# Reordering one projection step and the closing tiles of a fused attention and gating kernel

## The chip, the cores and the metric

The kernel runs on one core of a Trainium2 chip, as one launch. The metric is the device time of that launch in microseconds (us); less is better. The engines are named as the profile names them: PE (TensorE matmul), PEld (its weight loads), DVE (VectorE), ACT (ScalarE), POOL (GpSimd) and SP (SyncE, which here only issues DMAs).

## The reference

```python
xn = layernorm(A_x)                                   # 2048 x 640
# A: attention, 32 heads of 192, over the last W = 512 keys of the cache
q = (xn @ wq).heads()                                 # wq 640 x 6144
k, v = k_cache[:, :, -512:], v_cache[:, :, -512:]
p = softmax(q @ k.T * 192 ** -0.5)
s = (p @ v).merge_heads() @ wo                        # wo 6144 x 640
# B: two tokens (top 2 of xn @ w_r) go through a gated MLP; the others pass
b = xn; b[top2] += mlp(xn[top2]) * sigmoid(r[top2])
out = A_x + s * silu(b)                               # bfloat16
```

## The kernel before, in words

Every engine's instructions stand in an order that is written out by hand; the program's order of calls is the order on each engine's queue.

**Work items.** Heads are taken in 8 groups of four, and a group in two pairs of heads. A step is (group, 512 tokens, pair), 64 steps; each step has four token tiles of 128, so there are 256 items `m`, numbered through. For one `m` the kernel makes:

- scores (`scores`, L335 to L344): two heads, each a 128x512 bank of PSUM;
- the row maxima (`row_max`, L353, DVE), the exponentials (`exps`, L361, ACT, which also sum the rows) and a transpose of the exponentials by DMA, issued by SP (L366, `pT<-pexp`);
- P V (`o_products`, L378: 8 matmuls of 192 columns), whose result DVE scales by the reciprocal row sums into `o_sb` (`o_scaled`, L393), and a DMA transpose of `o_sb` (`o_turned`, L399, `oT<-o_sb`).

Beside these run two projections: `q_item` (L294), 5 matmuls of 512 columns for a third of a step's q, evacuated by ACT (L299); and `w_item`, the product with wo for 128 tokens of one group (`w_products`, L419: 12 matmuls of 320 columns in two halves), which DVE adds to `s_acc` (L437), or in the last group multiplies by the gate (`fin_t`, L442) and adds to `s_acc` (`fin_o`, L444). In the last stretch POOL also folds the gate and the residual into `s_acc` (L850, L851).

**PSUM.** `f_tile` deals out two banks in turn; q and P V both take them, so each user waits until the one before the last is evacuated. `w_banks` is one pair of banks for the wo product and for the scores of the first `m` of a unit. Four banks hold the other scores.

**Order.** From item 24 on the `m` are taken three at a time; such a triple is a unit `U` (12 to 88; unit 89 holds item 255 alone). For units 12 to 87 a loop plays the tokens of one string, STRETCH (L860): after the unit's scores, `M0` to `M5` are its six row maxima, `E0` to `E2` the exponentials of its three items, `R` the reciprocals of the unit before, `O1` one P V (of items one unit back), `q1` one q item, `W1` one wo product; `q`, `O`, `W` without a number are what is left of each (a unit has 3 P V, 2 or 3 q items, 1 or 2 wo products), `m`, `n`, `b` are pieces of part B, and `l` the loads. The exponentials of a unit's first two items share one transpose, which SP issues after `E1`; the third has its own after `E2`. The second P V of a unit reads the transpose that the unit before issued after its `E1`.

The closing part is a second string, LAST, played by `last` (L903): tokens `S`, `M`, `E`, `R` as above, `O.m` the P V matmuls of item `m`, `o.m` its scaling, `W.k` the wo product of token tile `k` in its last group (119 to 127; `.w` in `w_banks`, `.t` in a pair of banks that the scores have left, `.h` in an `f_tile` bank), `m.k` the product with the gate on DVE (L950), `g.k` or `a.k` the last addition on POOL or DVE (L954) and the store by SP (L955). `o` issues a transpose of its own item, except for items 252 and 255, which PE transposes (`T`, L411) and ACT copies (L413). `C` frees the score banks.

Of the kernel before, what the change touches and what calls it, by code (L numbers as in the profile page):

```python
# [9 lines left out]
ALU = mybir.AluOpType  # L10
AX = mybir.AxisListType
ET = mybir.EngineType
FP32 = mybir.dt.float32
BF16 = mybir.dt.bfloat16
# [7 lines left out]
def kernel(ctx, tc, A_x, A_k_cache, A_v_cache, A_wq, A_wo, B_x, B_w_r, B_w_gate, B_w_up, B_w_down, out):  # L22
    nc = tc.nc
    P = 128
    _, S, D = A_x.shape
# [3 lines left out]
    W = min(4096, max(256, Sk // 4))  # L29
# [9 lines left out]
    PAIRS = GROUP // 2  # L39
    CPG = GROUP * Dh // P  # L40
    DA = 512
    HD = D // 2
# [7 lines left out]
    out_v = out.flatten_outer_dims().rearrange("(n p) d -> p n d", p=P)  # L50
# [22 lines left out]
    def f_tile(shape, dtype, name):  # L73
        return ps_f.tile(shape, dtype, name=name, tag="f")

    xn = big.tile([P, NTB, D], BF16, name="xn")
    xnT = big.tile([P, NTB, DC, P], BF16, name="xnT")
    s_acc = big.tile([P, NTB, D], FP32, name="s_acc")
# [66 lines left out]
    for _ in range(22):  # L145
# [5 lines left out]
        out=ident_f, in_=ident_f, compare_op=ALU.not_equal, fill=1.0, base=0,  # L151
# [119 lines left out]
    steps = [(g, t5, pr) for g in range(NG) for t5 in range(NT5) for pr in range(PAIRS)]  # L271
    NS = len(steps)
    NM = 4 * NS
# [42 lines left out]
    def w_banks():  # L316

        if not wb:
            wb.extend(ps_w.tile([P, W], FP32, name=f"w_{c}", tag=f"w{c}") for c in range(2))
        return wb  # L320

    def scores(U):

        ms = units[U]
        tiles = {}
        for m in ms[1:] + ms[:1] if len(ms) == 3 else ms:
            g, t5, pr = steps[m // 4]
            ssl = slice((m % 4) * P, (m % 4 + 1) * P)
            if len(ms) == 3 and m == ms[0]:
                s0, s1 = w_banks()  # L330
            else:
                s0 = ps_sc.tile([P, W], FP32, name="s0", tag="sc")
                s1 = ps_sc.tile([P, W], FP32, name="s1", tag="sc")
            qT, kp = qT_of[m // 4], grp[g]["kT"][:, pr]
            nc.tensor.matmul(s0, lhsT=qT[:, 0, ssl], rhs=kp[:, :, 0, :], start=True, stop=False)  # L335
            nc.tensor.matmul(s1, lhsT=qT[:, 2, ssl], rhs=kp[:, :, 2, :], start=True, stop=False)  # L336
            tiles[m] = (s0, s1)
        for m in ms:
            g, t5, pr = steps[m // 4]
            ssl = slice((m % 4) * P, (m % 4 + 1) * P)  # L340
            s0, s1 = tiles[m]
            qT, kp = qT_of[m // 4], grp[g]["kT"][:, pr]
            nc.tensor.matmul(s0, lhsT=qT[0:64, 1, ssl], rhs=kp[0:64, :, 1, :], start=False, stop=True)  # L343
            nc.tensor.matmul(s1, lhsT=qT[64:128, 1, ssl], rhs=kp[64:128, :, 1, :], start=False, stop=True)  # L344
        return [tiles[m] for m in ms]
# [23 lines left out]
    def recip(U):  # L369
        n = 2 * len(units[U])  # L370
        nc.vector.reciprocal(out=l_of[U][:, 0:n], in_=l_of[U][:, 0:n])

    def o_products(m):
        g, t5, pr = steps[m // 4]
        o_ps = f_tile([P, 2, Dh], FP32, "o_ps")
        for hh in range(2):
            for j in range(NJ):
                nc.tensor.matmul(o_ps[:, hh, :], lhsT=pT_ring[:, m % RP, hh, j, :], rhs=grp[g]["v"][:, 2 * pr + hh, j, :],  # L378
                                 start=(j == 0), stop=(j == NJ - 1))
        return o_ps  # L380

    def o_slot(m):
        return (m if m < 2 * HEAD - 4 else m + 1) % RO

    def o_scaled(m, o_ps, act=False):
        U, a = unit_of[m]
        o_sb = o_ring[:, o_slot(m)]
        ls = l_of[U][:, 2 * a:2 * a + 2]
        if act:
            for hh in range(2):  # L390
                nc.scalar.activation(out=o_sb[:, hh], in_=o_ps[:, hh, :], func=ACT.Copy, scale=ls[:, hh:hh + 1])
        else:
            nc.vector.tensor_tensor(out=o_sb, in0=o_ps, in1=ls.unsqueeze(2).to_broadcast([P, 2, Dh]), op=ALU.mult)  # L393

    def o_turned(ms):

        n = len(ms)
        a, b = o_slot(ms[0]), (ms[0] + 1) % RT
        nc.sync.dma_start_transpose(out=oT_ring[:, b:b + n].rearrange("p u c t -> p (u c) t"),  # L399
                                    in_=o_ring[:, a:a + n].rearrange("p u h d -> p (u h d)"))  # L400
# [14 lines left out]
    def w_products(b, u, w_ps, part, off=0):  # L415

        wo_g = grp[steps[b * PAIRS][0]]["wo"]
        for c in range(CPG):
            nc.tensor.matmul(w_ps[:, part.start - off:part.stop - off], lhsT=oT_ring[:, (8 * b + 4 * (c // 3) + u + 1) % RT, c % 3, :],  # L419
                             rhs=wo_g[:, c, part], start=(c == 0), stop=(c == CPG - 1))  # L420

    fin_pool = {}
    tail_banks = []
# [168 lines left out]
    M = {}  # L592
# [264 lines left out]
        bg[109 + n].append(fin_pre(n))  # L857


    STRETCH = "M0 M1 R O1 E0 q1 M2 M3 E1 O1 M4 M5 E2 W1 m q1 n W q O b l".split()  # L860
    for token in FIRST:
        first(token)
    def q_until(s):
# [5 lines left out]
    for U in range(HEAD, NU - 2):  # L869
# [13 lines left out]
        tiles = scores(U)  # L883
        for token in STRETCH:
            if token[0] == "M":
# [14 lines left out]
    tail_ps = {}  # L900
    tail_sb = {}

    def last(token):  # L903


        op, *n = token.split(".")
        if op == "O":
            tail_ps[token[1:]] = o_products(int(n[0]))
        elif op == "o":
            o_scaled(int(n[0]), tail_ps[token[1:]])  # L910
            if int(n[0]) not in (NM - 4, NM - 1):
                o_turned([int(n[0])])
        elif op == "T":
            o_turn([int(m) for m in n])
        elif op == "R":
            recip(int(n[0]))
        elif op == "S":
            last_tiles[int(n[0])] = scores(int(n[0]))
        elif op == "M":
            row_max(int(n[0]), last_tiles[int(n[0])], int(n[1]))  # L920
        elif op == "E":
            exps(int(n[0]), int(n[1]), last_tiles[int(n[0])])
        elif op == "C":
            score_banks.close()
            tail_banks.append(pool("ps_t", 2, space=bass.MemoryType.PSUM))
        else:
            b, u = divmod(int(n[0]), 4)
            half = n[1] if len(n) > 1 and n[1] in "01" else None
            cs = slice(0, D) if half is None else slice(int(half) * HD, (int(half) + 1) * HD)
            g, t5, _ = steps[b * PAIRS]  # L930
            tok = t5 * 4 + u
            key = token[1:]
            if op == "W":
                key = "." + ".".join(n[:-1])
                if n[-1] == "t":
                    w_ps = tail_banks[0].tile([P, 2, W], FP32, name="w_t", tag="t")
                    w_ps = [w_ps[:, h, 0:HD] for h in range(2)]
                elif n[-1] == "w":
                    w_ps = [t[:, 0:HD] for t in w_banks()]
                else:  # L940
                    w_ps = {int(half): f_tile([P, HD], FP32, "w_e")}
                for h in range(2) if half is None else (int(half),):
                    w_products(b, u, w_ps[h], slice(h * HD, (h + 1) * HD), h * HD)
                tail_ps[key] = w_ps
            elif op == "m":
                if half is None or ("t", tok) not in tail_sb:
                    tail_sb["t", tok] = fin_pool["t"].tile([P, D], FP32, name="fin_t")
                for h in range(2) if half is None else (int(half),):
                    hs = slice(h * HD, (h + 1) * HD)
                    nc.vector.tensor_tensor(out=tail_sb["t", tok][:, hs], in0=tail_ps[key][h], in1=xn[:, tok, hs], op=ALU.mult)  # L950
            else:
                if half is None or ("o", tok) not in tail_sb:
                    tail_sb["o", tok] = fin_pool["o"].tile([P, D], BF16, name="fin_o")
                (nc.gpsimd if op == "g" else nc.vector).tensor_tensor(out=tail_sb["o", tok][:, cs], in0=tail_sb["t", tok][:, cs], in1=s_acc[:, tok, cs], op=ALU.add)  # L954
                nc.sync.dma_start(out=out_v[:, tok, cs], in_=tail_sb["o", tok][:, cs])  # L955

    LAST = """
    S.88 M.88.0 M.88.1 R.87 O.248 o.248 E.88.0 O.249 o.249 M.88.2 M.88.3 E.88.1 W.119.w m.119 O.250 o.250 M.88.4 M.88.5 E.88.2 g.119 W.120.w m.120 g.120 O.251 o.251
    S.89 M.89.0 M.89.1 E.89.0 R.88 C W.121.w m.121 g.121 O.252 o.252 W.122.w O.253 o.253 m.122 T.252 g.122 O.254 o.254 W.123.w m.123 g.123 R.89
    W.124.t m.124 g.124 O.255 o.255 W.125.w m.125 g.125 T.255 W.126.t m.126 g.126 W.127.0.h W.127.1.h m.127.0 m.127.1 a.127.0 a.127.1  # L960
    """.split()
    for token in LAST:
        last(token)
# [31 lines left out]
```

## Time and profile before

| what | us |
|---|---|
| three timed runs | 808.7, 811.0, 809.54 (median 809.54) |
| the profiled execution: its own time | 807.38 |
| its span in the trace | 805.6 |
| PE, busy with matmuls | 790.8 |
| DVE, busy | 624.1 |
| ACT, busy | 500.2 |
| POOL, busy | 217.4 |

The span is the time from the first instruction to the last in the trace of one execution; the execution's own time is 1.8 us more, for what lies around it. A busy PE is one with a matmul in its pipeline: matmuls overlap, so how densely they follow is read from the distance of their starts. The granted TensorE clock of the execution was 0.999 of full speed.

### The profile page before, as it was taken

Reading aid. Unit: us, or ns where it says so; the run is one execution under the profiler, and the core shown is the slowest. Engines: PE = TensorE matmul, PEld = TensorE weight load, DVE = VectorE, ACT = ScalarE, POOL = GpSimd, SP = SyncE. Lnnn points to the kernel's source line nnn. Section 1 sums busy time; section 2 is a strip of 40 time slices with the busy share of each in tenths; the row PEclk is TensorE's granted clock in tenths of the full one; section 3 lists DMA queues with packets and bytes.
Section 4 is the critical chain, followed back from the end, with each engine's and each line's share of the span. In section 5 each row is a group of like instructions: output and inputs, shape, how many; then the busy total and the mean of one; then the engine's idle time right before and its main releaser. Section 6 shows DMA issues by size and latency. Waiting matters only on the chain.

```text
span 805.6 us, 15848 instructions
## 1 busy us (share of the span) xinstructions
PE 790.8 (98%) x5776; PEld 483.2 (60%) x5776; DVE 624.1 (77%) x1303; ACT 500.2 (62%) x1281; POOL 217.4 (27%) x175
## 2 busy tenths in 40 slices
PE   8899999999999999999999999999999999999997
PEld 4456566666566665665665666666665565656665
DVE  7988778887787766777776777678888877668895
ACT  5777655665566665566655566557776666556651
POOL 0112000000000000000003899999900002452554
PEclk9999999999999999999999999999999999999999
DMA  8998999999799998899997996788888899897996
GB/s 219 189 176 167 195 203 168 173 174 189 160 203 195 200 198 162 187 199 191 206 184 151 188 199 138 154 174 174 172 159 152 164 183 188 166 156 145 176 156 133
DMA packets 441678, 142.31 MB, mean 177 GB/s; under 512 B 414500, under 2 KB 441256, under 8 KB 441600
## 3 DMA queue, kind: packets, MB, share of 16 engines
q1 hardware_dynamic: 439936, 138.79, 90.0%
q0 software_dynamic: 720, 1.70, 0.8%
q8 instruction: 45, 0.74, 0.4%
q10 hardware_dynamic: 944, 0.82, 0.3%
q14 instruction: 33, 0.27, 0.1%
HBM read 39.98 MB, written 2.62 MB: 53 GB/s over the span
## 4 chain that ended last, share of the span: by engine, by line
PE 89%; DMA 4%; DVE 3%; ACT 2%; issue 1%; DVEq 0%; SPq 0%; ACTq 0%
PE w L419 24%; PE q_ps L294 23%; PE o_ps L378 20%; PE s L336 4%; PE s L335 4%; PE s L343 4%; DMA pT<-pexp 4%; PE w L343 3%; PE w L335 2%; PE w L336 2%; DVE nm L353 2%; ACT pexp L361 1%; PE warm_ps L146 1%; DVE o_sb L393 0%; PE tp L267 0%
## 5 line engine op out<-in xcount | busy, mean ns | idle before, releaser
L361 ACT ACTIVATE pexp<-s,nm 128x512 bf16<-128x512 f32 x358 | 242.3, 684 | 14.9 <-DVE nm L353 10.5
L361 ACT ACTIVATE pexp<-w,nm 128x512 bf16<-128x512 f32 x154 | 104.5, 683 | 229.7 <-DVE nm L353 229.6
L353 DVE TENSOR_REDUCE nm<-s 128x1 f32<-128x512 f32 x358 | 228.6, 679 | 4.5 <-PE s L344 3.7
L294 PE MATMUL q_ps<-xnT,wq_g 128*128 128x512 bf16 x945 | 230.4, 379 | 0.1
L419 PE MATMUL w<-wo_g,oT 128*128 128x320 bf16 x1500 | 224.2, 299 | 0.0
L378 PE MATMUL o_ps<-v_sb,pT 128*128 128x192 bf16 x2048 | 211.1, 246 | 4.6 <-DMA pT<-pexp 3.2
L378 PEld LDWEIGHTS <-pT 128*128 128x128 bf16 x2048 | 169.1, 98 | 74.1 <-issue 36.6
L419 PEld LDWEIGHTS <-oT 128*128 128x128 bf16 x1536 | 148.6, 98 | 58.7 <-issue 0.9
L393 DVE TENSOR_TENSOR o_sb<-o_ps,lsum 128x384 bf16<-128x384 f32 x249 | 135.1, 543 | 55.5 <-PE o_ps L378 54.7
L353 DVE TENSOR_REDUCE nm<-w 128x1 f32<-128x512 f32 x154 | 99.1, 685 | 66.1 <-PE w L344 66.1
L294 PEld LDWEIGHTS <-wq_g 128*128 128x128 bf16 x945 | 91.0, 98 | 80.3 <-issue 1.1
L299 ACT ACTIVATE qT<-q_ps 128x512 bf16<-128x512 f32 x178 | 106.3, 597 | 22.2 <-PE q_ps L294 14.8
L437 DVE TENSOR_TENSOR s_acc<-s_acc,w 128x320 f32<-128x320 f32 x192 | 86.3, 479 | 28.1 <-PE w L419 28.0
L361 ACT ACTIVATION_READ_ACCUMULATOR pexp<-s,nm 128x1 f32 x358 | 72.0, 201 | 0.0
L336 PE MATMUL s<-kT,qT 128*128 128x512 bf16 x179 | 67.8, 379 | 1.4 <-ACT pexp L361 0.9
L335 PE MATMUL s<-kT,qT 128*128 128x512 bf16 x179 | 67.9, 379 | 0.6 <-ACT pexp L361 0.6
L794 POOL TENSOR_SCALAR yh<-y_bc,oh 128x640 bf16<-128x640 bf16 x32 | 60.5, 1892 | 2.9 <-DMA y_bc<-y_d 1.3
L780 POOL DMA_DIRECT2D y<-yp x4 | 2.1, 524 | 214.3 <-ACT yp L774 214.2
L343 PE MATMUL s<-kT,qT 64*128 64x512 bf16 x179 | 53.2, 377 | 0.0
L344 PE MATMUL s<-kT,qT 64*128 64x512 bf16 x179 | 53.2, 377 | 0.0
L343 PEld LDWEIGHTS <-qT 64*128 64x128 bf16 x256 | 17.1, 94 | 48.4 <-issue 38.4
L795 POOL TENSOR_TENSOR xn<-xn,yh 128x640 bf16<-128x640 bf16 x32 | 44.7, 1396 | 2.7
(148 smaller groups left out, 532.7 us busy)
## 6 DMA issues: line engine op xcount, KB each, us to landing
wo_g<-in_A_wo_dram SPq DMA_DIRECT2D x48, 160.0 KB, 2.9
wq_g<-in_A_wq_dram SPq DMA_DIRECT2D x35, 192.0 KB, 2.9
k_raw<-in_A_k_cache_dram SPq DMA_DIRECT2D x32, 192.0 KB, 3.4
v_sb<-in_A_v_cache_dram SPq DMA_DIRECT2D x32, 192.0 KB, 3.2
pT<-pexp SPq DMA_TRANSPOSE x169, 4.3
x_fin<-in_A_x_dram SPq DMA_DIRECT2D x16, 160.0 KB, 2.7
wgu<-in_B_w_gate_dram SPq DMA_DIRECT2D x15, 128.0 KB, 3.1
wgu<-in_B_w_up_dram SPq DMA_DIRECT2D x15, 128.0 KB, 3.1
```

The source lines that it names most:

```text
L294: nc.tensor.matmul(q_ps, lhsT=grp[g]["wq"][:, dc, col0:col0 + P], rhs=xnT[:, t5 * 4:(t5 + 1) * 4, dc, :], start=(dc == 0), stop=(dc == DC ...
L299: nc.scalar.activation(out=qT_of[i][:, c, :], in_=q_ps, func=ACT.Copy, scale=scale)
L335: nc.tensor.matmul(s0, lhsT=qT[:, 0, ssl], rhs=kp[:, :, 0, :], start=True, stop=False)
L336: nc.tensor.matmul(s1, lhsT=qT[:, 2, ssl], rhs=kp[:, :, 2, :], start=True, stop=False)
L343: nc.tensor.matmul(s0, lhsT=qT[0:64, 1, ssl], rhs=kp[0:64, :, 1, :], start=False, stop=True)
L353: nc.vector.tensor_reduce(out=nm_of[U][:, c:c + 1], in_=tiles[c // 2][c % 2], axis=AX.X, op=ALU.max, negate=True)
L361: nc.scalar.activation(out=p_ring[:, slot, hh, :], in_=tiles[a][hh], func=ACT.Exp, bias=nm_of[U][:, c:c + 1], scale=1.0, accum_out=l_of[U] ...
L378: nc.tensor.matmul(o_ps[:, hh, :], lhsT=pT_ring[:, m % RP, hh, j, :], rhs=grp[g]["v"][:, 2 * pr + hh, j, :], start=(j == 0), stop=(j == NJ ...
L393: nc.vector.tensor_tensor(out=o_sb, in0=o_ps, in1=ls.unsqueeze(2).to_broadcast([P, 2, Dh]), op=ALU.mult)
L419: nc.tensor.matmul(w_ps[:, part.start - off:part.stop - off], lhsT=oT_ring[:, (8 * b + 4 * (c // 3) + u + 1) % RT, c % 3, :], rhs=wo_g[:, ...
L437: nc.vector.tensor_tensor(out=s_acc[:, n, cs], in0=s_acc[:, n, cs], in1=w_ps[:, 0:HD], op=ALU.add)
L794: nc.gpsimd.tensor_scalar(out=yh, in0=M["y_bc"][:, j, :], scalar1=M["oh"][:, n, j:j + 1], scalar2=None, op0=ALU.mult)
```

## The change

1. In STRETCH the second `O1` and the `q1` behind the first wo product change places: the order scores, P V, q, P V, wo, q, ... becomes scores, P V, q, q, wo, P V, ... In each of the 76 units of the loop the second P V is issued behind the second q item and the wo product, and its scaling on DVE behind that of the wo product; ACT evacuates the second q item between `E1` and `E2`. SP's order in the loop is the same as before.
2. LAST is rewritten. Scaling and transposing are separate tokens (`o` and `U`): the closing items are transposed by DMA three, three and two at a time (248 to 250, 251 to 253, 254 and 255), and the PE transposes and ACT copies are gone. P V of two items stand together ahead of a wo product. The additions of tiles 120 and 122, of the first half of tile 126 and of the second part of tile 127 are on DVE, the others on POOL.
3. Stores are tokens of their own (`s`) and are issued by POOL (tiles 119, 121, 122), ACT (120, 123, 124, last part of 127) and SP (125, 126, first part of 127); before, all by SP.
4. The last tile is split in 384 and 256 columns, before in 320 and 320.

```diff
-    STRETCH = "M0 M1 R O1 E0 q1 M2 M3 E1 O1 M4 M5 E2 W1 m q1 n W q O b l".split()
+    STRETCH = "M0 M1 R O1 E0 q1 M2 M3 E1 q1 M4 M5 E2 W1 O1 m n W q O b l".split()
...
         elif op == "o":
             o_scaled(int(n[0]), tail_ps[token[1:]])
-            if int(n[0]) not in (NM - 4, NM - 1):
-                o_turned([int(n[0])])
+        elif op == "U":
+            o_turned([int(m) for m in n])
...
+            lc = LC if k == 4 * NS // PAIRS - 1 else HD
+            parts = [slice(0, lc), slice(lc, D)]
...
+            elif op in "ag":
+                if ("o", tok) not in tail_sb:
+                    tail_sb["o", tok] = fin_pool["o"].tile([P, D], BF16, name="fin_o")
+                (nc.gpsimd if op == "g" else nc.vector).tensor_tensor(out=tail_sb["o", tok][:, cs], in0=tail_sb["t", tok][:, cs],
+                                                                      in1=s_acc[:, tok, cs], op=ALU.add)
             else:
...
-                nc.sync.dma_start(out=out_v[:, tok, cs], in_=tail_sb["o", tok][:, cs])
+                queue = {"s": nc.sync, "p": nc.gpsimd, "a": nc.scalar}[n[-1]]
+                queue.dma_start(out=out_v[:, tok, cs], in_=tail_sb["o", tok][:, cs])
 
     LAST = """
-    S.88 M.88.0 M.88.1 R.87 O.248 o.248 E.88.0 O.249 o.249 M.88.2 M.88.3 E.88.1 W.119.w m.119 O.250 o.250 M.88.4 M.88.5 E.88.2 g.119 W.120.w m.120 g.120 O.251 o.251
-    S.89 M.89.0 M.89.1 E.89.0 R.88 C W.121.w m.121 g.121 O.252 o.252 W.122.w O.253 o.253 m.122 T.252 g.122 O.254 o.254 W.123.w m.123 g.123 R.89
-    W.124.t m.124 g.124 O.255 o.255 W.125.w m.125 g.125 T.255 W.126.t m.126 g.126 W.127.0.h W.127.1.h m.127.0 m.127.1 a.127.0 a.127.1
+    R.87 S.88 O.248 M.88.0 M.88.1 O.249 M.88.2 M.88.3 o.248 o.249 E.88.0
+    W.119.w O.250 E.88.1 M.88.4 M.88.5 O.251 o.250 m.119 S.89 M.89.0 E.88.2 M.89.1 g.119 s.119.p U.248.249.250
+    W.120.w E.89.0 C m.120 o.251 a.120 O.252 s.120.a
+    W.121.w R.88 R.89 O.253 o.252 m.121 o.253 O.254 g.121 s.121.p o.254
+    W.122.w m.122 O.255 a.122 U.251.252.253
+    W.123.w s.122.p o.255 m.123 U.254.255
+    W.124.w g.123 s.123.a m.124 g.124
+    W.125.t m.125
+    W.126.w m.126.0 s.124.a g.125 a.126.0 m.126.1 g.126.1 s.125.s
+    W.127.0.h m.127.0 s.126.s
+    W.127.1.h g.127.0 m.127.1 a.127.1 s.127.1.a s.127.0.s
     """.split()
```

More of the change, by code (lines that the diff above doesn't have):

```diff
@@ L901 @@
     tail_sb = {}
+    LC = 384
     def last(token):
@@ L926, in last @@
         else:
[L927 to L932, printed above, removed]
+            k = int(n[0])
+            b, u = divmod(k, 4)
+            tok = steps[b * PAIRS][1] * 4 + u
+            half = int(n[1]) if len(n) > 1 and n[1] in "01" else None
+            lc = LC if k == 4 * NS // PAIRS - 1 else HD
@@ L933, in last @@
+            parts = [slice(0, lc), slice(lc, D)]
+            cs = slice(0, D) if half is None else parts[half]
+            hs = range(2) if half is None else (half,)
             if op == "W":
-                key = "." + ".".join(n[:-1])
                 if n[-1] == "t":
-                    w_ps = tail_banks[0].tile([P, 2, W], FP32, name="w_t", tag="t")
-                    w_ps = [w_ps[:, h, 0:HD] for h in range(2)]
+                    w_t = tail_banks[0].tile([P, 2, W], FP32, name="w_t", tag="t")
+                    w_ps = [w_t[:, h] for h in range(2)]
@@ L938, in last @@
                 elif n[-1] == "w":
-                    w_ps = [t[:, 0:HD] for t in w_banks()]
+                    w_ps = w_banks()
                 else:
[L941 to L944, printed above, removed]
+                    w_ps = {half: f_tile([P, W], FP32, "w_e")}
+                for h in hs:
+                    w_products(b, u, w_ps[h], parts[h], parts[h].start)
+                    tail_ps[k, h] = w_ps[h]
@@ L945, in last @@
             elif op == "m":
-                if half is None or ("t", tok) not in tail_sb:
+                if ("t", tok) not in tail_sb:
                     tail_sb["t", tok] = fin_pool["t"].tile([P, D], FP32, name="fin_t")
-                for h in range(2) if half is None else (int(half),):
-                    hs = slice(h * HD, (h + 1) * HD)
-                    nc.vector.tensor_tensor(out=tail_sb["t", tok][:, hs], in0=tail_ps[key][h], in1=xn[:, tok, hs], op=ALU.mult)
-            else:
-                if half is None or ("o", tok) not in tail_sb:
-                    tail_sb["o", tok] = fin_pool["o"].tile([P, D], BF16, name="fin_o")
-                (nc.gpsimd if op == "g" else nc.vector).tensor_tensor(out=tail_sb["o", tok][:, cs], in0=tail_sb["t", tok][:, cs], in1=s_acc[:, tok, cs], op=ALU.add)
-                nc.sync.dma_start(out=out_v[:, tok, cs], in_=tail_sb["o", tok][:, cs])
+                for h in hs:
+                    nc.vector.tensor_tensor(out=tail_sb["t", tok][:, parts[h]], in0=tail_ps[k, h][:, 0:parts[h].stop - parts[h].start],
+                                            in1=xn[:, tok, parts[h]], op=ALU.mult)
+            elif op in "ag":
[3 more added lines that the diff above has]
+                                                                      in1=s_acc[:, tok, cs], op=ALU.add)
+            else:
+                queue = {"s": nc.sync, "p": nc.gpsimd, "a": nc.scalar}[n[-1]]
+                queue.dma_start(out=out_v[:, tok, cs], in_=tail_sb["o", tok][:, cs])
```

## The prediction

> **What bounds the kernel now.** I read the page first, for the shares of the engines.
>
> ```profile
> span 805.6 us, 15848 instructions
> ...
> PE 790.8 (98%) x5776; PEld 483.2 (60%) x5776; DVE 624.1 (77%) x1303; ACT 500.2 (62%) x1281; POOL 217.4 (27%) x175
> ```
>
> PE decides. Whether 98% leaves anything shows in the distance of matmul starts in the timeline: 0.216 us within q, 0.136 within wo, 0.083 within P V, the same in nearly every pair of neighbours between 104 and 776 us. The change adds and takes away no matmul there, so only places where PE stands still can be gained. The waits of PE and of its weight loads between 83 and 776 us name them (columns: total, times, longest):
>
> ```profile
> PEld L378 <- DMA pT<-pexp: 6.2, 9, 1.2
> ...
> PE o_ps L378 <- DMA pT<-pexp: 1.9, 5, 0.7
> PE o_ps L378 <- DVE o_sb L393: 0.7, 1, 0.7
> ```
>
> All of it is P V (L378). The timeline of one such unit shows which of the three:
>
> ```profile
> 378.67 1.24 PE L294 MATMUL q_ps<-xnT,wq_g 128*128 128x512 bf16 x5
> 380.61 0.83 PE L378 MATMUL o_ps<-v_sb,pT 128*128 128x192 bf16 x8 [0.70 <-DMA pT<-pexp]
> 381.28 1.79 PE L419 MATMUL w<-wo_g,oT 128*128 128x320 bf16 x12
> ```
>
> It is the second P V, behind the first q item. Five q starts take 1.08, so it could have begun at 379.75: 0.86 lost. (The view says 0.70, since it counts from the modelled end of a matmul.) By starts, seven units lose time to the transpose: at 287 us 0.54, 305 0.35, 379 0.86, 390 0.04, 671 0.57, 707 0.18, 744 0.42, together 2.96. Two more, at 643 (0.83) and 571 (0.08), have another cause:
>
> ```profile
> 642.80 1.24 PE L294 MATMUL q_ps<-xnT,wq_g 128*128 128x512 bf16 x5
> 644.71 0.82 PE L378 MATMUL o_ps<-v_sb,pT 128*128 128x192 bf16 x8 [0.67 <-DVE o_sb L393]
> ```
>
> Here the transpose had landed; the PSUM bank was still held by the first P V, because DVE was late with its scaling.
>
> Last the end, by the chain in order of time:
>
> ```profile
> 788.84 0.67 PE o_ps L378 x8
> ...
> 790.77 4.24 DMA pT<-pexp
> 795.05 0.83 PE o_ps L378 x8
> ...
> 797.52 0.17 PE tp_o L411 x3
> ...
> 801.41 0.93 DVE fin_o L954
> ```
>
> By starts PE loses 0.49 before item 254 and 0.96 before item 255, and each PE transpose takes 0.17. After the last matmul come two gate products, two additions, and the last store, issued at 802.92.
>
> **The stretch, units 12 to 87.** The order of instructions of the changed kernel shows the second P V moved on PE and its scaling on DVE in each unit, and SP's queue unchanged, so transposes and loads pass nothing new there. The matmuls per unit are the same.
>
> - The second P V starts 1.08 (q) + 1.63 (wo) = 2.7 us later. The longest late landing is 0.86, so the 2.96 goes. The third P V reads the same transpose and comes later still.
> - The second q item takes the old place of the second P V and the same bank, so it waits for the first P V's scaling as that did: the 0.83 and the 0.08 stay. Counted as nothing.
> - ACT evacuates the second q (597 ns, L299) between `E1` and `E2`. `E1` is not moved. The next user of that bank is the third q or the third P V. At 449.53 us, for example, it is a P V; `E1` is through at 448.2, the evacuation would end at 448.8, and P V finds the bank free. Over all units that slack comes to 0.60 us or more. `E2` moves back by up to 0.6; the next unit's scores need its bank at 450.84 there, and it would be through at 450.3. Hidden; if the cover is gone, each 0.1 us beyond it costs 7.6 us over 76 units.
> - DVE's row maxima `M4`, `M5` come one scaling earlier (0.46 apart in the queue), so the evacuation of wo, which they held up (PE gives its last matmul 0.42 later than before), ends as before. Whatever wo product follows needs the first bank 0.55 or more after that: hidden.
> - Behind the wo evacuation now waits the second scaling. In the last group `fin_o` (0.82) stands ahead of it. This bites only in unit 85, the one unit there with three q items: its third P V would start at 758.48, the bank comes free at about 758.86. Price +0.38.
>
> Stretch: -2.96 + 0.38 = -2.6.
>
> **The end, from the scores of unit 88 (775.54 in the old frame).** I laid the new order out by hand with the distances of starts above, 0.2 us from a matmul's last start to DVE, and on DVE 0.60 a row maximum, 0.52 a scaling, 0.40 a gate half and 0.82 an addition.
>
> - PE: P V 248, 249, wo 119, P V 250, 251, scores 89 end at 783.01. wo 120 needs the first `w` bank, which DVE, now with `M.88.4`, `M.88.5` and a scaling ahead of `m.119`, frees at 783.27: +0.26.
> - The transposes of 252 to 255 no longer queue behind four single transposes of `o_sb` (1.2 us each of SP, L399). With 3.2 us from issue to landing as in the closing part before, they land at 783.4, 784.8, 786.5 and 789.1; their P V come at 784.9, 787.2, 787.9 and 790.1. The 0.49 and the 0.96 go, and the two times 0.17 of PE transposes.
> - DVE, with the additions of 120 and 122, scales 255 only at 792.2 and frees the first bank for wo 124 at 792.66, PE being ready at 792.43: +0.25. The joint transpose of 251 to 253 is issued at 789.1. Nearest rows: 2.3 (three blocks) to 5.3 (nine blocks under load); I take 3.3, as the page's median says. It is needed at 793.1; at 5.3 it costs +1.3.
> - wo 127 then ends at 799.17 against 800.80: PE -1.6.
> - The additions on DVE beside POOL. The trace has this addition alone and beside one of POOL:
>
> ```profile
> 757.72 0.82 DVE L444 TENSOR_TENSOR fin_o<-fin_t,s_acc 128x640 bf16<-128x640 f32 x1
> ```
> ```profile
> 749.69 1.40 POOL L850 TENSOR_TENSOR s_acc<-s_acc,xn 128x640 f32<-128x640 f32 x1
> 750.25 1.54 DVE L444 TENSOR_TENSOR fin_o<-fin_t,s_acc 128x640 bf16<-128x640 f32 x1
> ```
>
> The second ends 0.70 after POOL's (751.09), and in the chain above the half addition of 0.93 ends 0.34 after POOL's (802.00), where its twin alone takes 0.48. So I let such an addition end 0.34 after POOL's. `a.126.0`, ready at 797.55, meets `g.125` (797.12 to 798.66) and ends at 799.0; behind it on DVE wait `m.126.1`, `m.127.0`, `m.127.1` (800.3). `a.127.1` meets `g.127.0` (800.35 to 801.27) and ends at 801.55. The stores leave at 801.35 and 801.6, against 802.92.
>
> The Trainium skill, page "SBUF — State Buffer", section "Who interferes with whom", calls the port that VectorE and GpSimd share an exclusive lock: a VectorE operation with two SBUF inputs and a GpSimd operation that reads SBUF never share it, and the loser waits for the whole instruction. The trace agrees (0.70 and 0.34 behind POOL's end). If both were merely slowed to 0.93 a half, the same layout would issue the last store at about 800.9, and the end would gain 2.0 instead of 1.2.
>
> - The last store on ACT's queue: the closing stores of SP landed 1.6 to 2.0 after issue; a load of ACT's queue, under load at the start, 4.0. I take 1.7, the row nearest in kind and place; the other end costs +2.3. Stores by POOL (0.58 of POOL each) are early, and no one waits for them.
>
> End: 802.92 - 801.6 = 1.3, less 0.1 for the queue: -1.2.
>
> **Sum.** -2.6 - 1.2 = -3.8. The profiled execution took 807.38 (span 805.6, the rest lies around it): 803.6. The timed runs lie higher, median 809.54, and I forecast in their frame: 805.7.
>
> **Rivals.**
> - The waits come back elsewhere. The busy share of the DMA engines between 83 and 300 us is 0.98; if they and not the place of one P V limit the rate, a gap closed here opens at another transpose. The end's 1.2 alone is left: 808.3. Against it: where PE does not wait, the landings come 0.3 to 4.2 us ahead of need and do not drift.
> - More waits than profiled. The median run is 2.2 us longer than the profiled one; if that is late landings, they go too: 803.5. For it: such waits are irregular. Against: nothing shows where those 2.2 lie.
> - The end gives back. The store on ACT's queue lands in 4.0: -3.8 + 2.3, 808.0.
> - Slower: the bank of the second q. Its slack of 0.60 is alike in all units, so one common delay of the evacuation behind `E1` hits all 76. It decides from 0.6 us; at 0.7 the price is 7.6, and 809.54 - 3.8 + 7.6 = 813.3. For it: ACT takes three q and exponentials in a row where it had two, and every one waits for DVE. Against: neither `E1` nor what it waits for moves.
> - That the change does not do what it says can be excluded: the order on the engines shows it.
>
> **How the numbers follow.** Runs of one kernel differ by about 0.3% (2.4 us; 808.7 to 811.0 here), which bounds "the same". Forecast (804.3 to 807.1) 0.50; more waits gone (803.5) 0.15; waits come back (808.3) 0.14; the end gives back (808.0) 0.11; slower 0.10. Faster: the first two and a part of the third and fourth that noise carries over, 0.68; same 0.21; slower 0.11. The range 803.2 to 808.6 takes in all but the slower case and the outer half of the second.
>
> **What would show it.** In the changed profile: no wait of L378 for `pT` between 83 and 776 us, and PE's span from the first scores of unit 12 to those of unit 88 shorter by 2.6; the wait for `o_sb` near 643 us now before a q matmul; about 0.38 of wait in unit 85; the last matmul 1.6 earlier against unit 88's scores; L958 on DVE stretched twice beside POOL; the last store near -1.3. It is wrong if waits for q's bank (ACT L299) appear in every unit, or if waits for DMA show before other matmuls.

## The result, and the profile after

| | before | after |
|---|---|---|
| timed, median (us) | 809.45 (808.7 to 811.0, 6 runs) | 805.60 (805.21 to 806.74, 6 runs) |
| profiled execution (us), its span | 807.38, 805.6 | 805.67, 803.9 |

The ratio is 0.9952, with a 95% interval of 0.9939 to 0.9965: 3.85 us faster, where 3.8 was forecast (805.7). The two profiled executions differ by 1.7 only.

The changed kernel's page opens as before's did; columns are busy time, share and instructions:

```profile
span 803.9 us, 15821 instructions
...
PE 790.2 (98%) x5770; PEld 483.7 (60%) x5770; DVE 643.8 (80%) x1305; ACT 486.3 (60%) x1279; POOL 217.6 (27%) x177
```

PE is as busy as it was; what can have changed is where it stands still. Its waits in the changed kernel between 83 and 776 us (total, times, longest), which answer to before's 6.2 + 1.9 for `pT`:

```profile
PE q_ps L294 <- DVE o_sb L393: 0.6, 2, 0.5
PE o_ps L378 <- DMA pT<-pexp: 0.5, 1, 0.5
PE o_ps L378 <- DVE o_sb L393: 0.3, 1, 0.3
```
```profile
PEld L378 <- DMA pT<-pexp: 0.9, 1, 0.9
```

The late transposes are gone but for one, and that one is unit 12's first P V at 87 us, which the change does not move. The wait for the first scaling has moved from P V (L378) to q (L294). It is the old one, at the same place; in the changed kernel's timeline:

```profile
642.29 1.24 PE L294 MATMUL q_ps<-xnT,wq_g 128*128 128x512 bf16 x5
644.00 1.24 PE L294 MATMUL q_ps<-xnT,wq_g 128*128 128x512 bf16 x5 [0.46 <-DVE o_sb L393]
```

By starts, 1.71 less 1.08 for five q matmuls, it is 0.63. DVE is late there because its gate operation (L802), beside POOL, took 1.77 and ended at 642.2, ahead of the unit's first maxima and that scaling.

To see where the time went I cut each trace at three matmuls: the first scores of unit 12, those of unit 88, and the first of wo 127 (us):

| kernel | start to unit 12 | unit 12 to 88 | unit 88 to wo 127 | wo 127 to the end |
|---|---|---|---|---|
| before | 83.69 | 691.85 | 23.63 | 6.43 |
| before, a second profile (e5) | 83.84 | 693.78 | 23.57 | 6.41 |
| after | 84.30 | 689.85 | 23.11 | 6.64 |
| stretch alone (e1) | 84.90 | 689.56 | 23.56 | 6.48 |
| end alone (e2) | 84.00 | 693.76 | 22.51 | 6.63 |
| tiles 119, 120 not stored (e3) | 84.72 | 690.24 | 21.82 | 6.72 |
| late stores, two more additions on DVE (e8) | 83.61 | 689.21 | 22.22 | 5.96 |

The code up to unit 12 is the same in all, and takes 83.6 to 84.9 here (85.6 in e7): a single profile decides nothing below 1 to 2 us over its whole span. The stretch gained 2.00 against before's first profile and 3.93 against its second, where 2.6 was forecast. The six profiles with the new stretch and the rest of the loop unchanged (after, e1, e3, e4, e7, e8) lie at 689.2 to 690.2, the three with the old one at 691.9 to 693.8. The end gained 0.31 (23.63 + 6.43 - 23.11 - 6.64), where 1.2 was forecast; in e2 it gained 0.92. Why the end gave so little is in its chain, in order of time:

```profile
784.51 5.52 DMA pT<-pexp
790.03 0.04 issue
790.07 0.83 PE o_ps L378 x8
790.90 3.26 PE w L419 x24
794.16 1.64 PE w_t L419 x12
...
795.90 0.77 DVE fin_t L953 x2
...
797.24 1.17 DVE fin_o L958
```

The transpose of item 255 was issued early (784.51), but took 5.52 to land, where the forecast had 3.2. PE stood 1.45 for it (by starts), more than the 0.96 that the change was to take away here. Below the last line the addition on DVE, which waits for POOL's, leads on to POOL's two additions of the last tiles (799.29 to 801.28) and to the last store behind them.

### The profile page after: what moved, and what is told of

It is laid out like the page before. It is cut to its first block, busy times and chain, and to the rows that moved or that the text cites. A ratio compares the mean times of both kernels' runs of the same rounds, so it can differ in the third digit from the quotient of the medians.

```text
span 803.9 us, 15821 instructions
## 1 busy us (share of the span) xinstructions
PE 790.2 (98%) x5770; PEld 483.7 (60%) x5770; DVE 643.8 (80%) x1305; ACT 486.3 (60%) x1279; POOL 217.6 (27%) x177
## 5 line engine op out<-in xcount | busy, mean ns | idle before, releaser
L353 DVE TENSOR_REDUCE nm<-s 128x1 f32<-128x512 f32 x358 | 222.6, 680 | 4.5 <-PE s L344 3.6
L294 PE MATMUL q_ps<-xnT,wq_g 128*128 128x512 bf16 x945 | 222.0, 379 | 0.7 <-DVE o_sb L393 0.6
L378 PE MATMUL o_ps<-v_sb,pT 128*128 128x192 bf16 x2048 | 207.6, 246 | 2.5 <-DMA pT<-pexp 1.7
L378 PEld LDWEIGHTS <-pT 128*128 128x128 bf16 x2048 | 169.1, 98 | 53.5 <-issue 36.0
L294 PEld LDWEIGHTS <-wq_g 128*128 128x128 bf16 x945 | 90.6, 98 | 89.0 <-issue 2.8
L299 ACT ACTIVATE qT<-q_ps 128x512 bf16<-128x512 f32 x178 | 106.9, 600 | 24.2 <-PE q_ps L294 16.9
L437 DVE TENSOR_TENSOR s_acc<-s_acc,w 128x320 f32<-128x320 f32 x192 | 92.7, 487 | 35.2 <-PE w L419 32.4
L361 ACT ACTIVATION_READ_ACCUMULATOR pexp<-s,nm 128x1 f32 x358 | 77.2, 216 | 0.0
```

The lines of the kernel that those rows point to most:

```text
L294: nc.tensor.matmul(q_ps, lhsT=grp[g]["wq"][:, dc, col0:col0 + P], rhs=xnT[:, t5 * 4:(t5 + 1) * 4, dc, :], start=(dc == 0), stop=(dc == DC ...
L299: nc.scalar.activation(out=qT_of[i][:, c, :], in_=q_ps, func=ACT.Copy, scale=scale)
L353: nc.vector.tensor_reduce(out=nm_of[U][:, c:c + 1], in_=tiles[c // 2][c % 2], axis=AX.X, op=ALU.max, negate=True)
L361: nc.scalar.activation(out=p_ring[:, slot, hh, :], in_=tiles[a][hh], func=ACT.Exp, bias=nm_of[U][:, c:c + 1], scale=1.0, accum_out=l_of[U] ...
L437: nc.vector.tensor_tensor(out=s_acc[:, n, cs], in0=s_acc[:, n, cs], in1=w_ps[:, 0:HD], op=ALU.add)
```

## The experiments

Each ratio is to the kernel before, timed in turn on the same chip. Where it has no interval, there was one run.

### The two halves

**e1**, STRETCH as changed, LAST and all else as before:

```diff
-    STRETCH = "M0 M1 R O1 E0 q1 M2 M3 E1 O1 M4 M5 E2 W1 m q1 n W q O b l".split()
+    STRETCH = "M0 M1 R O1 E0 q1 M2 M3 E1 q1 M4 M5 E2 W1 O1 m n W q O b l".split()
```

> The kernel before with the new order of the stretch and the old end. Theory A (the moved P V brings most): 2.0 to 3.5 us faster than before, no wait of L378 for pT left in units 13 to 87, and the end as before (PE's last product about 23.6 us behind the first scores of unit 88). Theory B (the end brings most): within 1.2 us of before.

Measured: 806.24 against 808.78, ratio 0.9961 [0.9949, 0.9974], 3.2 us by the ratio (2.5 by the medians). In its profile the only wait of L378 for `pT` in the loop is unit 12's, and unit 88 to wo 127 is as before, 23.56. Theory A holds.

**e2**, LAST as changed with its code, STRETCH as before (the diff above, reversed, on the changed kernel).

> The old order of the stretch with the new end. Theory A: 0.5 to 1.2 us faster than before, the waits of the second P V for pT as numerous as before. Theory B: 2.5 us faster or more. If the two parts are independent, the two gains add up to the 3.85 of the whole change.

Measured: 808.19, ratio 0.9989 [0.9979, 0.9998], 0.9 us (0.6 by the medians). The sum, 4.1 (3.1), agrees with the whole's 3.85 within the intervals, so nothing shows that the halves touch each other, and the stretch brings most.

### What before's profile did not show

**e5**, the kernel before, unchanged, profiled once more.

> The kernel before, unchanged, profiled a second time. The measured gain by the timed runs is 3.85 us, by the two profiled executions only 1.7. Theory M (the first profiled execution had few late landings): starts of the second P V in units 12 to 87 lose 4.0 us or more to the transpose of pexp, against 2.96 in the first profile. Rival N (the 2 us lie at the start or the end): they lose 2.5 to 3.3 and the difference shows before unit 12 or behind the scores of unit 88.

Measured: 809.41, span 807.6. Its waits between 83 and 776 us:

```profile
PE o_ps L378 <- DMA pT<-pexp: 3.3, 5, 0.9
```
```profile
PEld L378 <- DMA pT<-pexp: 8.2, 10, 1.4
```

They were 1.9 and 6.2. By starts, eight units lose 4.47 to a late transpose, where seven lost 2.96 in the first profile. Theory M holds. In e2, whose stretch is also the old one, it is 4.40. Counted by unit, the places are nearly the same in all three (us lost before the second P V):

| unit | 32 | 34 | 36 | 40 | 44 | 45 | 76 | 80 | 84 |
|---|---|---|---|---|---|---|---|---|---|
| before | - | 0.54 | 0.35 | - | 0.86 | 0.04 | 0.57 | 0.18 | 0.42 |
| e5 | 1.08 | 0.34 | 0.22 | - | 1.02 | 0.19 | 1.05 | 0.15 | 0.42 |
| e2 | - | 0.49 | 0.56 | 0.25 | 1.58 | - | 0.94 | 0.17 | 0.41 |

The times in the trace differ (unit 44's is at 380.61 in one trace, at 381.88 in the next), the units do not. So where a transpose lands late is set by the program; how late, and whether a close one tips over, differs from run to run. Unit 32's landed 0.09 ahead of need in the first profile. In the seven units of the first profile these transposes took 5.3 to 7.3 us to land, in most others 4.3 to 4.6; some others took over 5.3 and were still in time. What slows them was not tested. The first profile, of a run 1.3 us below the shortest timed one beside it (807.38 against 808.7), lost little. That is 1.5 of the 2.0 us between the two profiles, and most of why the timed gain is larger than the difference of the two first profiles.

### Why item 255's transpose took 5.5

Around it, in the changed kernel, POOL's and ACT's queues hold stores of tiles 119 and 120 (first time: issue). The transpose's issue on SP, with what stands near it on POOL and ACT:

```profile
784.51 1.36 SPq L366 DMA_TRANSPOSE pT<-pexp  x1
```
```profile
784.02 0.56 POOL L962 DMA_DIRECT2D out_dram<-fin_o  x1 [0.30 <-POOL fin_o L958]
```
```profile
785.32 9.75 ACTq L962 DMA_DIRECT2D out_dram<-fin_o  x2
```

Theory S: these stores, which the change issues early, slow the transposes beside them. Theory Q: the joint transpose of `o_sb` for 248 to 250 ahead of it on SP's queue does.

**e3** leaves out the stores of tiles 119 and 120, so those rows of the output are not written:

```diff
-    W.119.w O.250 E.88.1 M.88.4 M.88.5 O.251 o.250 m.119 S.89 M.89.0 E.88.2 M.89.1 g.119 s.119.p U.248.249.250
-    W.120.w E.89.0 C m.120 o.251 a.120 O.252 s.120.a
+    W.119.w O.250 E.88.1 M.88.4 M.88.5 O.251 o.250 m.119 S.89 M.89.0 E.88.2 M.89.1 g.119 U.248.249.250
+    W.120.w E.89.0 C m.120 o.251 a.120 O.252
```

> The changed kernel without the stores of tiles 119 and 120 (their rows of the output are left out). It asks why the transpose of item 255 took 5.5 us to land in the changed kernel where 3.2 was predicted, which holds PE up by 1.37 us. Theory S (the stores issued by POOL and ACT at 783.8 and 785.1 compete with it): it lands 3.2 to 3.6 us after its issue and the wait of PE before item 255 falls to 0.2 or less. Theory Q (it stands behind the joint transpose of 248 to 250 in one queue of DMAs): landing 5.0 to 5.6 and a wait of 1.2 to 1.4, as in the changed kernel.

Measured: 805.25. The transpose lands 3.21 after its issue, and P V of 255 follows without a wait:

```profile
789.43 0.82 PE L378 MATMUL o_ps<-v_sb,pT 128*128 128x192 bf16 x8
```

Unit 88 to wo 127 takes 21.82, against 23.11. The joint transpose stands ahead as it did, so alone it does not make item 255's late: theory S holds, Q as the only cause does not.

**e4** keeps the stores and splits the joint transpose, so that less stands ahead:

```diff
-    ... g.119 s.119.p U.248.249.250
-    W.120.w E.89.0 C ...
+    ... o.248 o.249 E.88.0 U.248.249
+    ... g.119 s.119.p
+    W.120.w E.89.0 U.250 C ...
```

> The changed kernel with the transpose of 248 to 250 taken apart: 248 and 249 together between the transposes of 252 and 253, 250 alone behind that of 254. Theory Q: the transpose of 255 lands about 4 us after issue, the wait before item 255 falls from 1.37 to 0.5 or less, and the run is 0.6 to 1.2 us faster than the changed kernel (4.5 to 5.0 faster than before). Theory S: the wait stays above 1.0 and the time within 0.4 us of the changed kernel.

Measured: 804.28, ratio 0.9937 [0.9924, 0.9950]. Item 255's transpose now lands 4.24 after issue and is in time, but 254's takes 4.51 and PE stands 1.18 for it; unit 88 to wo 127 is 23.30. By their letter theory Q's signs came (about 4, no long wait before 255, 4.5 to 5.0 us faster) and S's did not. But the delay went to the neighbour: 254's and 255's are the two transposes of exponentials issued within 1 us of the stores of 119 and 120. So e4 alone does not decide; e3 above and e7 below, where the joint transpose stays and the stores go, do. That what stands ahead adds to the delay when stores are in flight (5.52 behind the nine blocks of the joint one; 4.24 in e4, behind the eight of 254's, with 250's issued after it) is not excluded. The intervals of e4's ratio and the changed kernel's overlap, and in this profile what is shorter lies in the stretch, where the code is the same, so nothing is drawn from the time.

**e7** stores all tiles, but 119 to 122 by SP behind the last transposes (with six `fin_o` buffers for three):

```diff
-    ... g.119 s.119.p ...  s.120.a ...  s.121.p ...  s.122.p
+    W.122.w m.122 O.255 a.122 U.251.252.253 s.119.s s.120.s s.121.s
+    W.123.w o.255 m.123 U.254.255 s.122.s
```

> The changed kernel with the stores of tiles 119 to 122 issued by SP behind the joint transpose of 251 to 253 (that of 122 behind the one of 254 and 255), and fin_o with six buffers for three, so that no addition waits for a store. Theory S (the early stores delay the transpose of item 255): it lands 3.2 us after issue, no wait of PE before item 255, and the run is 0.9 to 1.5 us faster than the changed kernel, 4.8 to 5.4 faster than before. Rival (leaving the stores out helped because nothing was left to collide with; moved, they delay the transposes of 251 to 255 of o_sb instead): PE waits 0.5 us or more before the wo products of tiles 124 to 126 and the time is within 0.5 us of the changed kernel.

Measured: 804.89, ratio 0.9939 [0.9926, 0.9952]. 255 lands 3.16 after issue, no wait; unit 88 to wo 127 is 22.18, 0.93 less. Of this 0.35 is lost behind wo 127 (6.99), where DVE's addition of half of 126 again stands beside one of POOL, 1.57 long. One transpose is still late: item 251's, issued at 775.96 and landed 5.75 later, together with POOL's store of tile 118, which no version here moves. Theory S holds again for the wait. The time is 4.9 us below before by the ratio (4.4 by the medians), and the interval overlaps the changed kernel's, so a gain over that kernel is not shown by the time alone.

**e8** is e7 with the addition of 125 and both of 127 on DVE:

```diff
-    ... s.124.a g.125 a.126.0 m.126.1 ...
+    ... s.124.a a.125 a.126.0 m.126.1 ...
-    W.127.1.h g.127.0 m.127.1 a.127.1 s.127.1.a s.127.0.s
+    W.127.1.h m.127.1 a.127.0 a.127.1 s.127.0.s s.127.1.a
```

> As the kernel with late stores, and the additions of tile 125 and of the first part of tile 127 on DVE instead of POOL, so that the only one left on POOL at the end is the second half of tile 126. Theory L (an addition of DVE beside one of POOL waits for POOL's end, and this lengthens the end): no addition at L958 on DVE over 0.9 us, and the last store issued 0.3 to 0.6 us sooner behind PE's last product than in the kernel with late stores. Rival (DVE's own queue decides): the last store is issued at the same distance from it, within 0.2 us, or later.

Measured: 803.74, ratio 0.9930 [0.9918, 0.9942], span 801.0, the shortest of all here. The lock is gone from the end. First the changed kernel's half addition, then in e8 that of 125 and of half of 126 together:

```profile
797.24 1.51 DVE L958 TENSOR_TENSOR fin_o<-fin_t,s_acc 128x320 bf16<-128x320 f32 x1
```
```profile
794.90 1.21 DVE L958 TENSOR_TENSOR fin_o<-fin_t,s_acc 128x640 bf16<-128x640 f32 x2
```

The last store leaves 3.2 after the start of wo 127, in e7 4.1: 0.9 sooner, where 0.3 to 0.6 was expected. Not all of it is the lock. In e7 the last store also waits for two additions of POOL (799.54 to 801.57), and e8 takes one of them away; the two were not tested apart.

### The place of the second P V

**e6** moves it half as far, behind the second q item but ahead of the wo product:

```diff
-    STRETCH = "M0 M1 R O1 E0 q1 M2 M3 E1 q1 M4 M5 E2 W1 O1 m n W q O b l".split()
+    STRETCH = "M0 M1 R O1 E0 q1 M2 M3 E1 q1 O1 M4 M5 E2 W1 m n W q O b l".split()
```

> The changed kernel with the second P V behind the second q item but ahead of the wo product, so 1.08 us later than before the change and not 2.7. Theory A (late landings of up to 0.9 us, with rare ones over it): most of the waits go, 0 to 0.8 us of them stay in units 12 to 87, time within 0.6 us of the changed kernel. Rival (the whole 2.7 are needed): 1.5 us or more of waits for pT stay, and the time is 1.5 us or more above the changed kernel.

Measured: 833.35, ratio 1.0295 [1.0279, 1.0311]: 24 us slower than before. Neither theory had a place for that. Its waits of PE between 83 and 800 us begin with a new one, and a unit's timeline shows it, on PE and on DVE:

```profile
PE w L419 <- DVE s_acc L437: 18.8, 31, 0.6
```
```profile
469.06 1.79 PE L419 MATMUL w<-wo_g,oT 128*128 128x320 bf16 x12
471.47 1.79 PE L419 MATMUL w<-wo_g,oT 128*128 128x320 bf16 x12 [0.61 <-DVE s_acc L437]
```
```profile
469.26 0.56 DVE L393 TENSOR_TENSOR o_sb<-o_ps,lsum 128x384 bf16<-128x384 f32 x1 [1.01 <-PE o_ps L378]
469.74 1.28 DVE L353 TENSOR_REDUCE nm<-s 128x1 f32<-128x512 f32 x2
470.93 0.87 DVE L437 TENSOR_TENSOR s_acc<-s_acc,w 128x320 f32<-128x320 f32 x2
```

36 units with two wo products lose 0.77 each. Two readings: P V between two wo products is what covers the addition (C), or DVE's queue is at fault, where a scaling that waits 1.01 for PE stands ahead of two maxima that could run, and these ahead of the addition (D).

**e10** keeps DVE as in e6 and puts the third P V between the two wo products:

```diff
-    STRETCH = "M0 M1 R O1 E0 q1 M2 M3 E1 q1 O1 M4 M5 E2 W1 m n W q O b l".split()
+    STRETCH = "M0 M1 R O1 E0 q1 M2 M3 E1 q1 O1 M4 M5 E2 W1 m n q O W b l".split()
```

> As the halfway kernel (second P V behind the second q item and ahead of the wo product), but the third P V, and the third q item where there is one, stand between the two wo products of a unit, so that these no longer follow each other. Theory C (what cost 24 us in the halfway kernel is two wo products back to back, of which the second waits for DVE to add the first to `s_acc`; P V between them is its cover): the 0.77 in each unit with two wo products goes, and what is left of late transposes is what the halfway kernel had, about 0.6: within 1.5 us of the changed kernel, some 805 to 807. The next unit's scores need the wo banks 0.87 behind the second product, which about covers those 0.77. Theory D (the row maxima, which in the halfway kernel stand behind a scaling on DVE, are late, and with them the exponentials and the addition of wo, whatever stands between the wo products): still +15 or more, 820 to 833, with waits of wo or of scores for DVE.

Measured: 814.79, ratio 1.0082 [1.0063, 1.0100], between the two. The 36 waits shrink from 0.77 to 0.11, 4.0 in all, but in ten units the next scores, which use the same banks, wait for the late addition, another 5.9. So P V between hides the lateness in part; it does not explain it.

**e11** is e6 with the maxima ahead of the scaling; on PE, ACT, POOL and SP it is e6 instruction by instruction:

```diff
-    STRETCH = "M0 M1 R O1 E0 q1 M2 M3 E1 q1 O1 M4 M5 E2 W1 m n W q O b l".split()
+    STRETCH = "M0 M1 R O1 E0 q1 M2 M3 E1 q1 M4 M5 O1 E2 W1 m n W q O b l".split()
```

> As the halfway kernel on PE, ACT, POOL and SP, instruction by instruction; on DVE alone the row maxima `M4`, `M5` stand ahead of the second P V's scaling, as in the changed kernel, and not behind it. Wo products still stand back to back in the 37 units that have two. Theory D (the halfway kernel's +24 us come from DVE's queue: at 469.26 its scaling waited 1.01 for P V with two free maxima of 1.28 queued behind it, and behind those the addition that frees the first wo bank): the maxima then end near 469.4, the scaling near 469.9, and the first half of the wo product, through at 470.1, is added by 470.5, ahead of the second product at 470.7; the 0.77 goes in all units, 804 to 807. Theory C (two wo products back to back wait, because P V between them is the cover): 0.77 in 36 units stay, 830 or more. The kernel with the products apart, at 814.8, stands between the two: 0.11 of wait was left in each unit with two wo products, and in some 10 units the next scores waited about 0.57 for the wo banks.

Measured: 807.14, ratio 0.9967 [0.9954, 0.9980]. DVE and PE in a unit of two wo products:

```profile
473.55 2.48 DVE L353 TENSOR_REDUCE nm<-s 128x1 f32<-128x512 f32 x4
475.94 0.55 DVE L393 TENSOR_TENSOR o_sb<-o_ps,lsum 128x384 bf16<-128x384 f32 x1
476.72 0.49 DVE L437 TENSOR_TENSOR s_acc<-s_acc,w 128x320 f32<-128x320 f32 x1 [0.23 <-PE w L419]
```
```profile
475.64 3.42 PE L419 MATMUL w<-wo_g,oT 128*128 128x320 bf16 x24
```

The four maxima run through, the scaling has no wait, and DVE now waits for the wo product instead of the other way round. On PE the two products stand back to back, 24 matmuls without a gap, and nothing has to cover them. One exchange on DVE is worth 26 us; D holds, C falls as the cause. In this profile two transposes still come late for the second P V (0.69 and 0.60, in units 44 and 45 again): behind q alone it has less room than in the changed kernel, behind q and wo.

### The price of the rival that would have made it slower

**e9** lets ACT evacuate the second q item behind `E2` and not ahead of it (`p` its matmuls, `v` its evacuation):

```diff
-    STRETCH = "M0 M1 R O1 E0 q1 M2 M3 E1 q1 M4 M5 E2 W1 O1 m n W q O b l".split()
+    STRETCH = "M0 M1 R O1 E0 q1 M2 M3 E1 p1 M4 M5 E2 v1 W1 O1 m n W q O b l".split()
```

> As the changed kernel, but ACT evacuates the second q item behind the third item's exponentials (`E2`) where it did so ahead of them. It puts a price on the rival that would have made the change slower: the slack of the second q item's bank. In the changed trace the evacuation ends 0.74 us ahead of the next P V on that bank in a unit with one wo product (455.18 to 455.78 is such an evacuation; in the unit at 444 us it ends at 447.86, P V starts at 448.61) and 2.4 ahead in a unit with two (455.78 against 458.16); 39 of the 76 units have one, 37 have two. Two exponentials ahead delay it by 1.32. Theory B (the slack of 0.74 is real and each delay beyond it stops PE): 1.32 - 0.74, about 0.6, in each of 39 units with one wo product, none in the others: +23, some 828, the waits being of P V and the third q item for ACT's evacuation (L299). Theory R, as the prediction's rival had it, that the slack is alike in all units: 0.6 in 76, +45, some 850. Theory N (P V comes later than the bank asks for anyway, the slack is larger than it looks): within 1.5 of the changed kernel.

Measured: 830.38, ratio 1.0273 [1.0253, 1.0293]. The waits of PE (L304 is here what L299 is in the changed kernel) are of the two users named:

```profile
PE q_ps L296 <- ACT qT L304: 9.6, 20, 0.5
PE o_ps L388 <- ACT qT L304: 8.6, 18, 0.5
```

By starts it is 0.64 in each of 38 units with one wo product, 24.3 in all, and nothing in those with two. Theory B holds. The slack that the change leaves is real and short (1.32 - 0.64, about 0.7), in half of the units.

## Why the prediction was right, point by point

- **The late transposes in the stretch: right.** All seven places are free of waits. The size was that of one profile: 2.96, in a second one 4.47, mostly at the same units. The landings "0.3 to 4.2 us ahead of need" missed unit 32, at 0.09, which was late in e5.
- **The waits for the first scaling stay: right in kind.** 0.83 came out as 0.63, 0.08 as 0.34, and two more appeared (580 us 0.15, 752 us 0.10), each behind a DVE operation held up beside POOL. Unit 12's first P V, which no step of the change touches, lost 0.52 (0.23 and 0.43 in the profiles of before).
- **Unit 85: right.** Forecast 0.38, measured 0.46, and as said for the scaling behind `fin_o`:

```profile
757.09 0.74 PE L378 MATMUL o_ps<-v_sb,pT 128*128 128x192 bf16 x7 [0.30 <-DVE o_sb L393]
```

  Together these make -2.96 + 0.46 + 0.51 - 0.20 + 0.29 = -1.9 of the -2.00 between the first profiles.
- **The bank of the second q: right that it is hidden.** In the changed kernel's loop no matmul of q or P V waits for L299. The rival had two things wrong that e9 shows: the slack is not alike in all units (it is 2.4 where two wo products stand, so 38 units would pay and not 76), and it is some 0.7.
- **The maxima one scaling earlier: right, and worth more than it got.** The prediction saw that `M4`, `M5` hold up the addition of wo, and that this order moves them up. e6 and e11 show what it costs to leave the second P V's scaling ahead of them once P V itself is later: 24 us above before.
- **wo 120: right.** 0.26 forecast, 0.17 seen (0.49 between the starts, 0.32 in before).
- **The end's transposes: wrong.** The failed step is "With 3.2 us from issue to landing as in the closing part before". In the closing part before, all stores went by SP's own queue, the next one 1.35 us behind item 254's transpose and behind 255's. 254's landed in 3.07 with two stores in flight, but 255's took 4.24 with one, in a line which the prediction itself shows; why that one was slow is open (from 792.7 to 794.0 the DMA engines were busy but moved at most 28 GB/s, where during the 5.52 of the changed kernel they never moved under 97). The change puts stores of other queues ahead and beside, and "Stores by POOL ... are early, and no one waits for them" overlooked that a transpose waits with them. 3.2 became 5.52; of the forecast 1.6 on PE's way to wo 127 only 0.52 came. e3 and e7 give 1.81 and 1.45 when those stores are gone or late. The Trainium skill, page "DMA: Bandwidth & Descriptors", section "Issuing engines are not separate DMA queues", says that DMAs started by different engines run on the same 16 DMA engines and interleave. The traces agree (3.2 to 3.5 with no store in flight, 4.2 to 5.5 for those issued within 1 us of the stores of 119 and 120 in the changed kernel, e2 and e4). It was the rule to weigh when stores were moved to other queues.
- **The lock: right.** DVE's half addition began at 797.24, beside POOL's of 796.87 to 798.41, and ended 0.34 behind it, at 798.75; forecast 0.34. The second meeting did not stretch it: `a.127.1` began at 799.99 and took 0.44.
- **The last store on ACT's queue: right.** It landed 1.73 after issue; SP's took 1.6 to 1.8. (The prediction's 1.6 to 2.0 for before leaves out one closing store of SP, issued at 792.12, that took 3.40.)
- **When the last stores leave: wrong.** Counted from unit 88's first scores, ACT's left 26.31 behind them, forecast 26.06, and SP's 27.16, forecast 25.81; before it was 27.38. So the last store came 0.2 sooner and not 1.3, and it is SP's. Of the 1.35 that it is later than forecast, 1.08 is PE's (1.6 less 0.52); the rest lies behind PE, where it waited for POOL's two additions, which ended at 801.28.
- **The rivals.** "More waits than profiled" is true as a mechanism: e5 lost 1.5 more than the first profile, of the 2.2 that this rival asks for; with the end's 1.2 that would have been 804.2 and not 803.5. "The waits come back elsewhere" is excluded: nothing replaced them in the stretch, in e1 either. "The end gives back" came in part, but at the transposes and not at the last store.

So the total agrees more closely than its terms, and that is luck: 3.85 for 3.8. In the timed runs the stretch brought 3.2 (2.1 to 4.1) for 2.6, and the end 0.9 (0.2 to 1.7) for 1.2; both intervals hold the forecast. What shows that the terms were off, in opposite directions, are the profiles: the second profile of before for the stretch, item 255 for the end.

## What to carry to other kernels

A store moved to another engine's queue still shares the DMA engines: before moving it earlier, look which transfer on the critical path is in flight then. An instruction that waits for PE belongs behind whatever its in-order engine could already run; here one such exchange on DVE was worth 26 us, while the move of P V itself was worth 3. A second profile of the same kernel, compared unit by unit and not by time, tells which waits come back and how much their size differs; here they came back at the same units, at 2.96 and 4.47.

## What the runs showed that was not expected

- In the closing part, DMA transposes of 8 or 9 blocks (of 128 x 128) landed 3.2 to 3.5 us after issue with no store in flight (items 253 to 255 and the joint one of 248 to 250, in e3, e7 and e8), and in 4.2 to 5.5 when issued within 1 us of the 160 KB stores of tiles 119 and 120 (changed kernel, e2, e4). Not every store does it: in e4 the joint one of 251 to 253 took 3.30 with stores of POOL and ACT in flight, and in e7 and e8 3.2 with three of SP's issued 1.4 us or more behind it.
- Two kernels that are the same on every engine but DVE, and there differ by one place in the queue (e6, e11), lie 26 us apart.
- The lowest time seen is e8's, 803.74 (0.9930, an interval that just touches the changed kernel's): the changed kernel with the first four stores behind the transposes and two more of the last additions on DVE.
